# The last batch of a gated MLP with spatial mixing: four pieces of 272 columns instead of 276, and the streamed operands of TensorE moved to other addresses

## The chip, the cores and the metric

One core of a Trainium2 chip. The metric is the device time of one execution in microseconds (us); smaller is better. Three runs of the kernel before took 318.91, 319.26 and 319.99 us, median 319.26 us.

## What is computed

```python
# attention without softmax, B=4 batches, H=4 heads, S=1088 tokens, head_dim 32
phi(x)  = outer(S1 @ x, S2 @ x).reshape(64)
out     = phi(q) @ (phi(k).T @ v) / (phi(q) @ sum(phi(k)) + 1e-6)
x       = heads joined                                  # [B, 1088, 128]
# gated MLP, d_ff = 1024
h       = relu(x @ w_in); u, v = h[..., :512], h[..., 512:]
v_n     = layer norm of v
v_s     = einsum('ts,bsd->btd', w_spatial, v_n) + b_spatial   # W is 1088 x 1088
result  = (u * v_s) @ w_out                             # [B, 1088, 128]
```

Everything must hold to float32 accuracy, so each large product is made of float32r matmuls on a high and a low part: a·b is a_hi·b_hi + a_lo·b_hi + a_hi·b_lo, three matmuls.

## The kernel before

The work runs batch after batch. While TensorE (PE) mixes the tokens of batch b, the attention of batch b+1 is prepared on the other engines and put between its matmuls. The order of every operation on every engine is a list of numbers in the source (ORDER, one number for each recorded operation); the program issues them in that order and adds the semaphores.

**W.** Transposed W lies in SBUF as tile wT, high parts (wTh) and low parts (wTl), 9 row blocks of 128 tokens (NS), a row of PITCH = 1152 floats. Its 1088 columns are three chunks CH, chunk 1 with 332 columns, chunk 0 with 424, chunk 2 with 332. AT tells where each lies in a row: chunk 1 at 0, chunk 0 at 332, then a gap of 12 floats (GAP, filled with zeros by two POOL operations at L584), and chunk 2 at 768.

**Batches 0 to 2** (main, L927 on) take the columns by these chunks: for each d (four blocks of 128 features) and chunk, hidden makes u (3 matmuls into bank pu), spatial runs 26 matmuls into bank sp (L1041, L1043, L1050, L1052), gate multiplies and splits (DVE, ACT), and out_mm multiplies by w_out (3 matmuls into bank po). In each of these matmuls the streamed ("moving") operand is a row of 332 or 424 floats: of wT in spatial, of x in hidden, of the tile g in out_mm. The 128 x 128 operand that is loaded first ("stationary") is a block of v, w_in or w_out.

**The last batch** (main_fast, L1216 on) makes the mixing of two feature blocks with 7 block products instead of 8: W is cut into 2 x 2 blocks, 512 tokens by half of the columns, and sums of such blocks are made ahead from W's columns, which are loaded again from HBM (weights_fast: block, L1172; halves, L1182; less after it). Each half is two pieces CW of 276 columns:

```python
CW = (276, 276)
FROM = ((0, 276), (548, 824))
```

The last 64 tokens are a remainder of two matmuls (L1325, L1326). Since 1088 columns and the gap of 12 are cut into four pieces of 276, the third piece (548 to 823) holds 4 columns that the second has too, 204 columns, the gap, and 56 columns. REAL says which of its columns are real: hidden and out_mm use 260 there, and gate multiplies it in two parts, 204 and 56 columns. All in all main_fast issues 464 matmuls, 336 in product (L1313 to L1315), 32 in the remainders, 48 in hidden (helper L460 to L462), 48 in out_mm (L1402 to L1404); 440 of them stream 276 columns, 24 stream 260.

**Where the operands lie.** All tiles have fixed places in SBUF, one after the other in the order in which the code asks for them, so the start of each streamed operand modulo 64 bytes can be worked out. The code has small pads (pad0 to pad4, and `[:, 4:]` on wT) that shift these starts by 16 or 32 bytes. In the kernel before they are:

| streamed operand | columns | start modulo 64 bytes |
|---|---|---|
| wT, chunks 1 and 2; g | 332 | 48 |
| wT, chunk 0; g, chunk 0 | 424 | 32 |
| x, chunk 1; x, chunk 2 | 332 | 32; 48 |
| x, chunk 0 | 424 | 16 |
| last batch: wT, block sums, x, gates | 276, 260 | 0, 16, 32 and 48, mixed |

The stationary operands start at 32 modulo 64, but for those of attention's 384- and 320-column matmuls (0) and four of the last batch's remainders (48).

Of the kernel before, what the change touches and what calls it, by code (L numbers as in the profile page):

```python
# [9 lines left out]
F32 = mybir.dt.float32  # L10
F32R = mybir.dt.float32r
# [8 lines left out]
P = 128  # L20
# [10 lines left out]
AT = [332, 0, 768]  # L31
PITCH, G_PITCH, G_AT = 1152, 448, {424: 0, 332: 52}
GAP = slice(756, 768)
CW = (276, 276)
FROM = ((0, 276), (548, 824))
HALF = sum(CW)
REAL = (((0, [(0, 276)]), (276, [(0, 276)])), ((552, [(4, 204), (220, 56)]), (812, [(0, 276)])))
SEGS = (0, 276, 332, 548, 552, 768, 824, 828, 1104)
# [51 lines left out]
0 1 2 3 4 5 10 13 14 11 6 12 15 56 37 7 8 16 17 18 19 20 21 22 59 60 61 43 44 45 39 po0 47 48 49 27 28 29 30 31 32 23 po1 po1 po1 po1 68 41 51 69 52 58 70 65 38 40 53 42 57 202 46  # L90
50 66 9 24 54 71 62 203 211 178 193 187 175 102 63 33 101 207 190 181 67 55 103 34 72 35 64 81 82 73 74 75 92 79 76 90 212 36 213 204 214 80 77 78 215 91 83 194 188 179 116 117 112
120 84 216 85 217 86 218 118 113 93 87 219 88 94 114 121 119 182 89 115 95 122 104 191 176 96 123 141 124 220 125 97 133 126 105 142 143 134 352 127 353 189 135 128 144 137 129 138
139 136 366 367 98 99 205 221 106 100 206 210 208 109 131' 381 184 382 154 140 130 145 285 132 177 146 147 286 162 396 148 155 291 163 297 180 107 199 149 292 158 159 290 287 289
293 150 108 196 164 288 294 295 298' 296 302 299 301 300 160 165 156 152 157 161 151' 303 153' 185 304 166 167 168 169 170 171 305 307 306 308 309 315 172' 200 321 222 310 312 311
313 197 195 316 314 320 186 322 318 183 173' 327 192 174 326 317 333 323 319 325 328 249 336 255 256 324 329 338 331 332 341 209 372 339 330 373 342 374 375 387 223 201 340 388 389
# [1475 lines left out]
```

## Time and profile before

| | |
|---|---|
| median of three runs | 319.26 us |
| the profiled execution: its own time | 319.49 us |
| its span, first to last instruction | 317.7 us |
| PE busy | 312.8 us, 98% of the span |
| DVE, ACT, POOL busy | 237.7, 172.9, 48.4 us |
| granted TensorE clock | 0.999, full speed (2.4 GHz) |

The profile calls a matmul busy from its start to the modelled end of its pipeline, and matmuls overlap. The busy time of one (290 ns for 276 columns) is thus not what it costs in a stream; that is the distance from its start to the start of the next, which the timeline shows.

### The profile page before, as it was taken

To read this page: it belongs to the slowest core of one execution; us is meant where nothing else is said; L and a number is where in the kernel's file an instruction comes from. 1 tells how busy PE (TensorE), PEld (TensorE's weight loads), DVE (VectorE), ACT (ScalarE), POOL (GpSimd) and SP (SyncE) were. 2 spreads that over 40 slices of the span, in tenths; PEclk is the share of its full clock that TensorE was granted. 3 is DMA by queue.
4 is the path that set the end of the run, shared out by engine and by line. 5 is a ranking of instruction groups with operands and counts; after the bars stand their busy time and mean duration, and the time that the engine had idled before them with its cause. 6 is when DMAs were issued, how large, how long until landed. Compare 5 with 4: busy or idle time off the path is not lost.

```text
span 317.7 us, 7096 instructions
## 1 busy us (share of the span) xinstructions
PE 312.8 (98%) x2717; PEld 299.4 (94%) x2717; DVE 237.7 (75%) x551; ACT 172.9 (54%) x424; POOL 48.4 (15%) x63
## 2 busy tenths in 40 slices
PE   8999999999999999999999999999999999999996
PEld 7877999999999999999889999999999999999995
DVE  5999997365787956468895789879987987863445
ACT  2599956445774354465636557653154468442432
POOL 2000100765500001642002342100000000000000
PEclk9999999999999999999999999999999999999999
DMA  6952255637113036620113432423121333210001
GB/s 192 325 164 55 77 173 179 210 114 217 45 52 96 12 99 163 166 79 0 50 33 109 138 115 78 121 59 85 53 73 53 92 99 108 78 39 2 0 2 70
DMA packets 26019, 30.77 MB, mean 97 GB/s; under 512 B 3330, under 2 KB 25730, under 8 KB 25986
## 3 DMA queue, kind: packets, MB, share of 16 engines
q1 hardware_dynamic: 25986, 30.33, 32.2%
q8 instruction: 21, 0.34, 0.5%
q14 instruction: 12, 0.10, 0.1%
HBM read 27.25 MB, written 3.06 MB: 95 GB/s over the span
## 4 chain that ended last, share of the span: by engine, by line
PE 95%; DMA 3%; DVE 1%; SPq 1%; issue 0%; DVEq 0%
PE sp L1041 16%; PE sp L1043 14%; PE sp L1050 14%; PE sd L460 4%; PE sd L461 4%; PE sd L462 4%; PE pu L460 3%; PE sd L1313 3%; PE sd L1315 3%; PE sd L1314 3%; PE pu L461 2%; PE pu L462 2%; PE po L460 2%; PE sp L1313 2%; PE sp L1315 2%; PE sp L1314 2%
## 5 line engine op out<-in xcount | busy, mean ns | idle before, releaser
L1041 PE MATMUL sp<-wT,vh 128*128 128x332 f32 (+1 forms) x306 | 98.9, 324 | 0.0
L1043 PE MATMUL sp<-wT,vl 128*128 128x332 f32 (+1 forms) x272 | 87.7, 322 | 0.0
L1050 PE MATMUL sp<-wT,vh 128*128 128x332 f32 (+1 forms) x272 | 86.0, 321 | 0.0
L1041 PEld LDWEIGHTS sp<-wT,vh 128*128 128x128 f32 x306 | 57.5, 188 | 1.8 <-issue 0.8
L1043 PEld LDWEIGHTS sp<-wT,vl 128*128 128x128 f32 x272 | 51.1, 188 | 0.6
L1050 PEld LDWEIGHTS sp<-wT,vh 128*128 128x128 f32 x272 | 51.1, 188 | 0.1
L1077 DVE TENSOR_TENSOR u<-sp,u 128x332 f32<-128x332 f32 (+1 forms) x32 | 16.7, 522 | 17.9 <-PE sp L1052 7.9
L899 DVE BATCH_NORM_STATS2 small<-vt 128x6 f32<-128x512 f32 x36 | 24.1, 682 | 6.7 <-ACT vt L897 6.7
L897 ACT ACTIVATE vt<-sd 128x512 f32<-128x512 f32 x36 | 21.4, 599 | 11.7 <-PE sd L462 10.9
L877 DVE RECIPROCAL area<-area 128x384 f32<-128x384 f32 (+1 forms) x9 | 21.8, 2419 | 7.0 <-ACT area L875 7.0
L816 POOL TENSOR_TENSOR area<-area 128x384 f32<-128x384 f32 (+1 forms) x18 | 17.3, 970 | 57.6 <-DVE vh L966 26.5
L543 ACT CAST g<-u 128x332 fp32r<-128x332 f32 (+1 forms) x32 | 15.5, 487 | 18.0 <-DVE u L1077 9.4
L1033 ACT ACTIVATE u<-pu 128x332 f32<-128x332 f32 (+1 forms) x32 | 14.9, 466 | 11.0 <-PE pu L462 9.7
L473 POOL TENSOR_TENSOR area<-area,area 128x384 fp32r<-128x384 f32 (+1 forms) x18 | 18.0, 1005 | 19.5 <-ACT area L543 10.8
L470 DVE TENSOR_TENSOR g<-u,g 128x332 fp32r<-128x332 f32 (+1 forms) x32 | 17.1, 533 | 2.4 <-ACT g L543 1.4
L630 DVE TENSOR_TENSOR area<-ka,sd 128x768 f32<-128x768 f32 x15 | 13.7, 946 | 4.7 <-ACT ka L628 4.6
L595 ACT CAST wT<-area 128x332 fp32r<-128x332 f32 (+1 forms) x27 | 12.4, 497 | 8.0 <-DMA area<-in_wT 7.9
L460 PE MATMUL pu<-x,wih 128*128 128x332 f32 (+3 forms) x52 | 16.7, 320 | 0.0
L461 PE MATMUL pu<-x,wih 128*128 128x332 f32 (+3 forms) x52 | 16.3, 314 | 0.0
L462 PE MATMUL pu<-x,wil 128*128 128x332 f32 (+3 forms) x52 | 16.3, 314 | 0.0
L919 DVE TENSOR_SCALAR vt<-vt,small 128x512 f32<-128x512 f32 x31 | 15.9, 536 | 0.0
L957 ACT CAST vh<-vt 128x384 fp32r<-128x384 f32 x24 | 12.1, 516 | 6.8 <-DVE vt L919 6.8
(240 smaller groups left out, 765.4 us busy)
## 6 DMA issues: line engine op xcount, KB each, us to landing
w<-in_wT SPq DMA_DIRECT2D x48, 138.0 KB
area<-in_wT SPq DMA_DIRECT2D x18, 166.0 KB
area<-in_vA SPq DMA_DIRECT2D x12, 198.0 KB
area<-in_kT SPq DMA_DIRECT2D x12, 192.0 KB
area<-abd SPq DMA_DIRECT2D x24, 96.0 KB
area<-abd SPq DMA_DIRECT2D x12, 192.0 KB
area<-in_wT SPq DMA_DIRECT2D x9, 212.0 KB
area<-in_qT SPq DMA_DIRECT2D x7, 192.0 KB
```

The lines of the kernel that those rows point to most:

```text
L460: nc.tensor.matmul(o, ah, bh, start=start, stop=False)
L461: nc.tensor.matmul(o, ah, bl, start=False, stop=False)
L462: nc.tensor.matmul(o, al, bh, start=False, stop=stop)
L470: return lambda: nc.vector.tensor_tensor(out=o(), in0=a(), in1=bb(), op=ALU.subtract)
L473: return lambda: nc.gpsimd.tensor_tensor(out=o(), in0=a(), in1=bb(), op=ALU.subtract)
L816: op("POOL", c_pool(n), lambda fa=fa, fb=fb: nc.gpsimd.tensor_tensor(out=fa[:, :n], in0=fa[:, :n], in1=fb[:, :n], op=ALU.mult), r=[fb], w= ...
L877: op("DVE", 135 + 6.3 * n, lambda x32=x32, n=n: nc.vector.reciprocal(out=x32[:, :n], in_=x32[:, :n]), w=[x32])
L897: op("ACT", c_act(512, True) + 16, lambda pv=pv, t=t: nc.scalar.activation(vt[:, t], pv.ap, AF.Relu), r=[pv], w=[(vt, toks(t))])
L899: op("DVE", 690, lambda stats=stats, t=t: nc.vector.bn_stats(out=stats.ap, in_=vt[:, t]), r=[(vt, toks(t))], w=[stats])
L1041: nc.tensor.matmul(sp[:, :cw], vh[:, kt], wTh[:, kt, cs], start=(kt == 0), stop=False)
L1043: nc.tensor.matmul(sp[:, :cw], vl[:, kt], wTh[:, kt, cs], start=False, stop=False)
L1050: nc.tensor.matmul(sp[:, :cw], vh[:, kt], wTl[:, kt, cs], start=False, stop=False)
```

## The change

It cuts the 1088 columns into four pieces of exactly 272 (0, 272, 544, 816), with no gap, no column taken twice, and no partial piece. Chunk 2 of wT moves from 768 to 756. The two POOL operations that zero the gap go. Tiles g, x, the block sums and two stationary tiles (vd0, vd1) are shifted by a few floats.

```diff
-AT = [332, 0, 768]
-PITCH, G_PITCH, G_AT = 1152, 448, {424: 0, 332: 52}
-GAP = slice(756, 768)
-CW = (276, 276)
-FROM = ((0, 276), (548, 824))
+AT = [332, 0, 756]
+PITCH, G_PITCH, G_AT = 1152, 448, (0, 4, 8)
+CW = (272, 272)
+FROM = ((0, 272), (544, 816))
 HALF = sum(CW)
-REAL = (((0, [(0, 276)]), (276, [(0, 276)])), ((552, [(4, 204), (220, 56)]), (812, [(0, 276)])))
-SEGS = (0, 276, 332, 548, 552, 768, 824, 828, 1104)
+SEGS = (0, 272, 332, 544, 756, 816, 1088)
...
-    homes["x"] = const.tile([P, 2, SB_BUFS["xh"], SPAD], F32R, name="x")
+    wide = 2 * SB_BUFS["xh"] * SPAD
+    homes["x"] = const.tile([P, 24 + wide], F32R, name="x")[:, 12:12 + wide].rearrange("p (n i c) -> p n i c", n=2, i=SB_BUFS["xh"])
...
-    homes["vd1", 0] = homes["wi1"][:, HALF + CW[0]:HALF + CW[0] + P]
+    homes["vd1", 0] = homes["wi1"][:, 840:840 + P]
...
-            homes.update({("gf", i): flat[:, i * CW[1]:(i + 1) * CW[1]] for i in range(4)})
-            homes["vd0", 0] = flat[:, 4 * CW[1]:4 * CW[1] + P]
+            homes.update({("gf", i): flat[:, 4 + i * CW[1]:4 + (i + 1) * CW[1]] for i in range(4)})
+            homes["vd0", 0] = flat[:, 1104:1104 + P]
...
-            at = G_AT[t.shape[1]]
-            return homes["g"][:, t.slot, at:at + t.shape[1]]
+            at = t.slot * G_PITCH + G_AT[int(t.name[-1])]
+            return homes["g"][:, at:at + t.shape[1]]
...
-    for t in (wTh, wTl):
-        def blank(t=t):
-            z = z9[:, :NS * 12].rearrange("p (k c) -> p k c", k=NS)
-            return nc.gpsimd.tensor_tensor(out=t[:, :, GAP], in0=z, in1=z, op=ALU.subtract)
-        op("POOL", 360, blank, r=[z9], w=[tl(None, f"gap_{t.name}", [1, 1]), (t, "gap")], due=8000)
...
-                parts = [(lambda: g[:, 0, :cw], (g, 0)), (lambda: g[:, 1, :cw], (g, 1))]
+                parts = [(lambda: g[:, 0, 12:12 + cw], (g, 0)), (lambda: g[:, 1, 12:12 + cw], (g, 1))]
...
-        at = [0, 0, 0]
+        at = [4, 12, 12]
...
         def real(half, c):
-            at, parts = REAL[half][c]
-            return at, sum(n for _, n in parts), parts
+            return FROM[half][c], CW[c], [(0, CW[c])]
```

The starts modulo 64 bytes are then:

| streamed operand | columns | start modulo 64 bytes |
|---|---|---|
| wT, g, x of chunk 1 | 332 | 48 |
| wT, g, x of chunk 2 | 332 | 0 |
| wT, g, x of chunk 0 | 424 | 32 |
| last batch: all 464 matmuls | 272 | 48 |

The stationary operands of the last batch all start at 32 modulo 64. Those of the 512-column matmuls of hidden_v, which are taken from x, move from 32 to 48.

The list ORDER is rewritten from end to end, since six operations go and all later numbers fall. PE, ACT and SP issue what they issued before in the same order, with 272 columns where 276 or 260 stood. On DVE four operations less are issued, all in the last batch. One place of DVE's order there before (w, u, g, vt are tiles in SBUF, sd a PSUM bank, the number behind a name tells its buffer; at the end of a row stand partitions by elements):

```order
L1378 TENSOR_TENSOR w_2260<-sd_93,w_2260 128x276
L1390 TENSOR_TENSOR u_250<-w_2260,u_250 128x204
L1138 TENSOR_TENSOR g<-u_243,g 128x276
L1390 TENSOR_TENSOR u_250<-w_2260,u_250 128x56
L1138 TENSOR_TENSOR vt<-vt 128x4x128 x2
L1138 TENSOR_TENSOR w_2254<-w_2254,w_2258 128x276
```

and with the change:

```order
L1370 TENSOR_TENSOR w_2258<-sd_93,w_2258 128x272
L1380 TENSOR_TENSOR u_250<-w_2258,u_250 128x272
L1131 TENSOR_TENSOR g<-u_243,g 128x272
L1131 TENSOR_TENSOR vt<-vt 128x4x128 x2
L1131 TENSOR_TENSOR w_2252<-w_2252,w_2256 128x272
```

One multiplication of 272 columns stands where two of 204 and 56 stood. The other place of this kind is POOL's start of the work on W, before:

```order
L500 CAST v_87<-first 64x128
L988 ISA
L988 TENSOR_TENSOR vl<-vt,vh 128x512
L584 TENSOR_TENSOR wT<-first 128x9x12 x2
L598 TENSOR_TENSOR wT<-area_79,wT 128x332 x5
L816 TENSOR_TENSOR area_79<-area_79 128x384
```

and with the change:

```order
L500 CAST v_87<-first 64x128
L981 ISA
L981 TENSOR_TENSOR vl<-vt,vh 128x512
L591 TENSOR_TENSOR wT<-area_79,wT 128x332 x5
L809 TENSOR_TENSOR area_79<-area_79 128x384
```

The two operations that zero the gap are gone, and nothing else moved.

## Rows read from the trace of the kernel before

**Rows 1.** The page: span, busy time by engine, the chain that ended last.

```profile
span 317.7 us, 7096 instructions
PE 312.8 (98%) x2717; PEld 299.4 (94%) x2717; DVE 237.7 (75%) x551; ACT 172.9 (54%) x424; POOL 48.4 (15%) x63
PE 95%; DMA 3%; DVE 1%; SPq 1%; issue 0%; DVEq 0%
```

**Rows 2.** Windows: busy us (xcount) of PE, PEld, DVE, ACT, POOL; clock; DMA.

```profile
254.80:314.60 59.80, 59.80 (x468) 59.26 (x466) 38.36 (x94) 28.80 (x80) 0.00 (x0) 1.00 0.16 47
```

**Rows 3.** Timeline of PE, last batch: start us, busy us, line, operands, columns.

```profile
282.83 0.29 PE L1315 MATMUL sp<-later,vh 128*128 128x276 f32 x1
...
286.13 0.29 PE L1313 MATMUL sd<-wT,vh 128*128 128x276 f32 x1
...
307.77 0.28 PE L460 MATMUL pu<-x,wih 128*128 128x260 f32 x1
...
308.13 0.29 PE L1313 MATMUL sd<-wT,vh 128*128 128x276 f32 x1
```

**Rows 4.** Timeline of PE, a stream of 332 columns at 48 after 512-column matmuls.

```profile
214.05 0.31 PE L1041 MATMUL sp<-wT,vh 128*128 128x332 f32 x1
...
216.79 0.31 PE L1041 MATMUL sp<-wT,vh 128*128 128x332 f32 x1
...
217.67 0.31 PE L1041 MATMUL sp<-wT,vh 128*128 128x332 f32 x1
```

**Rows 5.** Timeline of PE, x of chunk 2 (at 48) inside such a stream.

```profile
233.14 0.31 PE L1050 MATMUL sp<-wT,vh 128*128 128x332 f32 x1
233.29 0.31 PE L460 MATMUL pu<-x,wih 128*128 128x332 f32 x1
...
234.02 0.31 PE L1050 MATMUL sp<-wT,vh 128*128 128x332 f32 x1
```

**Rows 6.** Timeline of PE: x chunk 1 (at 32), 424 columns, x chunk 0 (at 16).

```profile
236.66 0.32 PE L460 MATMUL pu<-x,wih 128*128 128x332 f32 x1
...
237.12 0.35 PE L1041 MATMUL sp<-wT,vh 128*128 128x424 f32 x1
...
238.80 0.36 PE L460 MATMUL pu<-x,wih 128*128 128x424 f32 x1
...
239.97 0.35 PE L1041 MATMUL sp<-wT,vh 128*128 128x424 f32 x1
```

**Rows 7.** Timeline of PE, DVE and ACT around the tightest supply in the last batch.

```profile
269.15 0.29 PE L1314 MATMUL sp<-later,vl 128*128 128x276 f32 x1
268.32 0.68 DVE L1138 TENSOR_TENSOR vl<-vt,vh 128x512 fp32r<-128x512 f32 x1
262.28 0.39 ACT L1368 COPY w<-sd 128x276 f32<-128x276 f32 x1 [1.68 <-PE sd L1315]
```

**Rows 8.** Operations of DVE and POOL that go: by form, and POOL's timeline.

```profile
L1390 DVE TENSOR_TENSOR u<-w,u 128x204 f32<-128x204 f32 x2 | 0.7, 371 | 0.2
L1390 DVE TENSOR_TENSOR u<-w,u 128x56 f32<-128x56 f32 x2 | 0.4, 209 | 0.0
55.32 0.69 POOL L584 TENSOR_TENSOR wT<-first 128x108 fp32r<-128x108 f32 x2 [21.49 <-DVE x L470]
```

**Rows 9.** Timeline of PE, DVE and ACT at the end.

```profile
312.39 0.29 PE L1326 MATMUL sd<-wT,wi 128*128 128x276 f32 x1
312.51 0.29 PE L1402 MATMUL po<-g,woh 128*128 128x276 f32 x1
312.78 0.45 DVE L1384 TENSOR_TENSOR u<-sd,u 128x276 f32<-128x276 f32 x1 [0.18 <-PE sd L1326]
313.26 0.42 ACT L1397 CAST later<-u 128x276 fp32r<-128x276 f32 x1 [0.84 <-DVE u L1384]
313.71 0.45 DVE L1138 TENSOR_TENSOR later<-u,later 128x276 fp32r<-128x276 f32 x1
314.21 0.39 PE L1404 MATMUL po<-later,woh 128*128 128x276 f32 x1
```

More of the change, by code (lines that the diff above doesn't have):

```diff
@@ L89 @@
 ORDER = """
[L90 to L95, printed above, removed]
[42 rows of a table removed]
+0 1 2 3 4 5 10 13 14 11 6 12 15 54 35 7 8 16 17 18 19 20 21 22 57 58 59 41 42 43 37 po0 45 46 47 25 26 27 28 29 30 23 po1 po1 po1 po1 66 39 49 67 50 56 68 63 36 38 51 40 55 200
+44 48 64 9 24 52 69 60 201 209 176 191 185 173 100 61 31 99 205 188 179 65 53 101 32 70 33 62 79 80 71 72 73 90 77 74 88 210 34 211 202 212 78 75 76 213 89 81 192 186 177 114
+115 110 118 82 214 83 215 84 216 116 111 91 85 217 86 92 112 119 117 180 87 113 93 120 102 189 174 94 121 139 122 218 123 95 131 124 103 140 141 132 350 125 351 187 133 126 142
+135 127 136 137 134 364 365 96 97 203 219 104 98 204 208 206 107 129' 379 182 380 152 138 128 143 283 130 175 144 145 284 160 394 146 153 289 161 295 178 105 197 147 290 156
+157 288 285 287 291 148 106 194 162 286 292 293 296' 294 300 297 299 298 158 163 154 150 155 159 149' 301 151' 183 302 164 165 166 167 168 169 303 305 304 306 307 313 170' 198
+319 220 308 310 309 311 195 193 314 312 318 184 320 316 181 171' 325 190 172 324 315 331 321 317 323 326 247 334 253 254 322 327 336 329 330 339 207 370 337 328 371 340 372 373
[43 rows of a table added]
 """
@@ L371, in tile_kernel @@
     const.tile([P, 4], F32, name="pad3")
-    first = const.tile([P, SB_BUFS["g"] * G_PITCH], F32, name="first", tag="garea", bufs=1)
+    first = const.tile([P, SB_BUFS["g"] * G_PITCH - 24], F32, name="first", tag="garea", bufs=1)
     fixed["z9"], fixed["sk_e"] = first[:, :P], first[:, P:P + NSK]
-    homes["x"] = const.tile([P, 2, SB_BUFS["xh"], SPAD], F32R, name="x")
+    wide = 2 * SB_BUFS["xh"] * SPAD
+    homes["x"] = const.tile([P, 24 + wide], F32R, name="x")[:, 12:12 + wide].rearrange("p (n i c) -> p n i c", n=2, i=SB_BUFS["xh"])
     homes |= {(t, i): homes["x"][:, n, i] for n, t in enumerate(("xh", "xl")) for i in range(SB_BUFS[t])}
@@ L415, in gates @@
         if "g" not in homes:
-            flat = const.tile([P, SB_BUFS["g"] * G_PITCH], F32R, name="g", tag="garea", bufs=1)
-            homes["g"] = flat.rearrange("p (n c) -> p n c", c=G_PITCH)
-            homes.update({("gf", i): flat[:, i * CW[1]:(i + 1) * CW[1]] for i in range(4)})
-            homes["vd0", 0] = flat[:, 4 * CW[1]:4 * CW[1] + P]
+            flat = const.tile([P, SB_BUFS["g"] * G_PITCH - 24], F32R, name="g", tag="garea", bufs=1)
+            homes["g"] = flat
+            homes.update({("gf", i): flat[:, 4 + i * CW[1]:4 + (i + 1) * CW[1]] for i in range(4)})
+            homes["vd0", 0] = flat[:, 1104:1104 + P]
     def place(t):
@@ L424, in place @@
         if t.tag == "ge":
-            return later(0)[:, t.slot * CW[1]:(t.slot + 1) * CW[1]]
+            return later(0)[:, 4 + t.slot * CW[1]:4 + (t.slot + 1) * CW[1]]
         if t.name in ("wTh", "wTl"):
@@ L1155, in weights_fast @@
                     if (j, i, n, c) == (4, 3, 1, 0):
-                        pieces[j, i, n, c] = (lambda: homes["wi1"][:, HALF:HALF + CW[0]]), [(t, (j, i, n, c)) for t in (wih[1], wil[1])]
+                        pieces[j, i, n, c] = (lambda: homes["wi1"][:, 12 + HALF:12 + HALF + CW[0]]), [(t, (j, i, n, c)) for t in (wih[1], wil[1])]
                         continue
@@ L1163, in weights_fast @@
             cs = slice(CW[0] * c, CW[0] * c + CW[c])
-            pieces[2, 1, 1, c] = (lambda cs=cs: homes["wi1"][:, cs]), [(t, (2, 1, 1, c)) for t in (wih[1], wil[1])]
+            pieces[2, 1, 1, c] = (lambda cs=cs: homes["wi1"][:, 12 + cs.start:12 + cs.stop]), [(t, (2, 1, 1, c)) for t in (wih[1], wil[1])]
             for i in range(4):
@@ L1168, in weights_fast @@
                         pieces[2, i, n, c] = (lambda i=i, n=n, cs=cs: sx[i - 2][:, n * HALF + cs.start:n * HALF + cs.stop]), [(sx[i - 2], (n, c))]
-                    t, a = (wTh, wTl)[n], SEGS[4] + CW[0] * c
+                    t, a = (wTh, wTl)[n], FROM[1][c]
                     pieces[3, i, n, c] = (lambda i=i, t=t, a=a, c=c: t[:, i, a:a + CW[c]]), [(t, cols(i, a, CW[c]))]
```

85 rows, old and new, of the table ORDER are left out of this document.

## The prediction

> **What bounds the kernel now.** The page comes first. PE is busy 98% of the span, and PE is 95% of the chain that ended last [rows 1]. The windows say it for the last batch: from 254.80 to 314.60 us PE is busy all of the 59.80 us, in 468 matmuls, at the full clock, while DVE fills 38.36 us and ACT 28.80 [rows 2]. So what counts is how long one matmul holds PE, and the timeline tells it as the distance between starts. In the last batch the first and the last start shown are 26 matmuls of 276 columns apart: (286.13 − 282.83) / 26 = 126.9 ns [rows 3]. A matmul of 260 columns holds it (308.13 − 307.77) / 3 = 120 ns [rows 3].
>
> The reader should then compare these with the columns alone, at 2.4 per ns: 276 columns are 115.0 ns, so 11.9 ns are extra, 10.3%. In a long stream of 332 columns (138.3 ns) the extra is smaller, but only after a while. From 214.05 to 216.79 are 18 matmuls of 152.2 ns (extra 10%), and the next six, to 217.67, have 146.7 ns (extra 6.0%) [rows 4]. I call the first state unsettled and the second settled. Nothing differs between them but the time since the stream began: the same line, tile and address. For 424 columns (176.7 ns) nine settled matmuls, 237.12 to 238.80, have 186.7 ns (extra 5.7%) [rows 6].
>
> Two things decide whether a stream settles. The first is the start address. Three matmuls on x of chunk 2, which start at 48 modulo 64 as the stream around them does, cost (234.02 − 233.14) / 6 = 146.7 ns on average, so they don't disturb it [rows 5]. Three on x of chunk 1, at 32 between streams at other addresses, cost (237.12 − 236.66) / 3 = 153 ns [rows 6]. Three on x of chunk 0, at 16, cost with the three of out_mm that follow them (239.97 − 238.80) / 6 = 195 ns instead of 186.7 [rows 6]. The second is the length. 146.7 ns are 22 steps of 6.67 ns (16 columns' time at 2.4 GHz), and 186.7 are 28 such steps. A stream settles, as I read it, where the time that a matmul wants, about 1.06 of its columns' time, is a whole number of such steps, so that the next one starts as the last did. For 276 columns, 1.06 × 115.0 = 121.9 ns lies between 18 steps (120.0) and 19 (126.7): they can't settle, and have 126.9.
>
> **The change, part by part.**
>
> (a) *The last batch.* All 464 matmuls get 272 columns and one start, 48. Their columns take 113.3 ns, and 1.06 × 113.3 = 120.1 ns is 18 steps. No row shows 272 columns. The bounds: below, the ratio of settled 424 (186.7 / 176.7), 119.8 ns; above, the ratio of 276 now (126.9 / 115.0), 125.1 ns. I take 120.0, since 332 and 424 settle within a percent of that ratio where the steps fit. 440 matmuls go from 126.9 to 120.0. The six of them that start after 312.39 don't count, since there PE waits for the last gate [rows 9]: 434 × 6.9 = 3.0 us less. The 24 of 260 columns stay at 120 ns: 0.
>
> (b) *Supply.* With PE faster, what is late next? The closest delivery is at 269.15, where PE takes the low part that DVE finished at 268.32 + 0.68 = 269.00 [rows 7]; 0.15 us of room. PE would come about 122 matmuls × 6.9 ns = 0.84 us earlier. ACT's and DVE's work for it hangs on a PE result at 262.28 [rows 7], which itself comes 0.47 us earlier. That leaves 0.84 − 0.47 − 0.15 = 0.2 us of waiting. Bounds: 0 and 0.7 (if DVE doesn't move). +0.2 us.
>
> (c) *The 332-column streams of batches 0 to 2.* This is the price. Until now all of wT and g at 332 columns starts at 48; with the change chunk 1 starts at 48 and chunk 2 at 0, and the order puts them in turn. In the order of PE's queue the 768 matmuls of 332 columns stand in 39 unbroken runs of one address now and in 101 with the change, 62 more, most of them of 3 matmuls. An unsettled matmul costs 152.2 − 146.7 = 5.5 ns more [rows 4]; three of them 16.5 ns; 62 × 16.5 = +1.0 us. Below, 0: a move by 16 bytes might cost nothing at equal length. Above, if nothing at 0 ever settles: 384 × 5.5 = +2.1 us.
>
> (d) *x of chunk 0 goes from 16 to 32*, the address of its stream. The six matmuls at 195 ns cost 6 × 8.3 = 50 ns more than settled ones [rows 6]; I count only the three on x, since the stream after them is often cut by something else anyway: 25 ns for each of 11 such runs, −0.27 us. Bounds: −0.1 (the stream is unsettled there in most places) and −0.55 (all six).
>
> (e) *What costs nothing.* POOL's two zeroings took 0.69 us at 55.32 after 21.49 us of idling [rows 8]; the cover is POOL's 15% load. DVE loses four operations; (371 + 209) ns become some 445 [rows 8, 9], 0.5 us in all on an engine with a third of the last batch free [rows 2]. The end, from the remainder's matmul at 312.39 through DVE 0.45, ACT 0.42, DVE 0.45 to the last matmul and its store [rows 9], has 4 columns less in each: under 0.02 us. The 512-column matmuls keep their moving operand; their stationary one goes from 32 to 48, and no row shows whether that counts.
>
> Sum: −3.0 + 0.2 + 1.0 − 0.27 = −2.1 us. The profiled execution took 319.49 us, 0.23 over the median of 319.26; against the median the forecast is **317.2 us**.
>
> **The rivals.**
>
> *Only columns count.* [...] As a mechanism of this kernel: from 260 to 276 columns the distance grows by 6.9 / 16 = 0.43 ns a column [rows 3], so 272 take 125.2. The gain is 440 × 1.7 − 24 × 5.2 = 0.6 us, the other streams stay: **318.6 us**. Against it stands the drop from 152.2 to 146.7 at equal columns [rows 4]. Chance 0.12.
>
> *272 doesn't settle*, because what it wants is a little over 18 steps (by a line through the settled 332 and 424, whose extras are 8.3 and 10.0 ns, it would be 120.6). Then it takes about 125 too, −0.6, and the streams of 332 pay +1.0, less 0.27: **319.4 us**. Chance 0.17.
>
> *Slower: chunk 2 at 0 never settles.* The only rows with starts at 0 and 48 in turn are the mixed 276s, all unsettled. Then (c) is 2.1 us, paid over three batches, and with (d) that is +1.85. It decides for a slower kernel where the last batch brings under 0.9 us, that is where 272 takes over 124.9 ns; at 125.2, **320.5 us**. For it: every new address here is untried. Against it: 424 settles at 32 and 332 at 48, so no single address is needed. Chance 0.09. With 272 settled and chunk 2 not, −3.0 + 0.2 + 2.1 − 0.27 = −1.0, **318.3 us**; chance 0.06.
>
> **How the numbers follow.** The forecast has 0.56. Its own range is 316.2 (switches free, no waiting) to 317.9 (0.7 us of waiting or dearer switches). To hold 8 in 10, I reach to 319.6, over the first two rivals and the last; 320.5 and some hundredths below 316.2 are left out. A measurement tells about 0.3% (0.96 us) from no change, so faster is below 318.3. Faster: the forecast and half of the 318.3 case, 0.59, say 0.60. Same: 318.6, 319.4 and the other half, 0.31. Slower: 0.09.
>
> **What would show it.** In the timeline of the changed kernel the last batch's starts should be 120.0 ns apart within some 15 matmuls and stay so; 125 would prove (a) wrong, and with it most of the forecast. The window of the 468 matmuls should last some 57 us instead of 59.80. A run at 0 of more than 15 matmuls at 332 columns should come down to 146.7 ns; if it stays at 152, the slower rival's mechanism is there. Three-matmul groups at a foreign address should cost about 152 each. A gap before a matmul near 266 to 269 us, released by DVE, would show (b). The end behind the last remainder should keep its length.

## The result, and the profile after

The changed kernel took 321.3 us (median of six runs, 320.76 to 322.0), the kernel before 319.14 us beside it (six runs). The ratio is 1.0064, with a 95% interval of 1.0047 to 1.0081: **slower by some 0.6%**, where 317.2 us and a gain of 0.6% had been forecast. 321.3 lies above the range too. The profiled execution took 322.0 us.

The page of the changed kernel looks like the one before [rows 1]: PE is still the bound, and its busy time grew by 1.1 us.

```profile
span 320.2 us, 7086 instructions
PE 313.9 (98%) x2717; PEld 300.7 (94%) x2717; DVE 236.8 (74%) x547; ACT 172.9 (54%) x424; POOL 47.7 (15%) x61
PE 96%; DMA 2%; SPq 1%; DVE 0%; issue 0%
```

The window of the last batch, with the same 468 matmuls as [rows 2], comes 3 us later and is only 0.6 us shorter, not 3:

```profile
257.95:317.15 59.20, 59.20 (x468) 58.69 (x466) 37.86 (x90) 28.75 (x80) 0.00 (x0) 1.00 0.16 47
```

The timeline of PE tells why. Columns: start us, busy us, line, operands, columns streamed. First, 26 matmuls out of the last batch. From the first start shown to the second it is (286.08 − 282.82) / 26 = 125.4 ns for one. The forecast was 120.0; the 276 columns before had 126.9 [rows 3].

```profile
282.82 0.29 PE L1308 MATMUL sp<-later,vh 128*128 128x272 f32 x1
...
286.08 0.29 PE L1308 MATMUL sp<-later,vh 128*128 128x272 f32 x1
```

Now two long streams of 332 columns, the first on W's chunk 1 (start 48 modulo 64), 37 matmuls, the second on chunk 2 (start 0), 26 matmuls, each up to the next operand:

```profile
62.19 0.31 PE L1034 MATMUL sp<-wT,vh 128*128 128x332 f32 x1
...
67.61 0.32 PE L460 MATMUL po<-g,woh 128*128 128x332 f32 x1
...
205.22 0.32 PE L1034 MATMUL sp<-wT,vh 128*128 128x332 f32 x1
...
209.20 0.31 PE L460 MATMUL pu<-x,wih 128*128 128x332 f32 x1
```

(67.61 − 62.19) / 37 = 146.5 ns: settled from its first matmul. (209.20 − 205.22) / 26 = 153.1 ns: not settled to its end, though 26 matmuls are more than the 18 after which the stream of [rows 4] came down.

Where the time went: from the first 512-column matmul to the first one of the last batch the kernel before took 235.24 us, the changed one 237.51: **+2.27**. From there to the last matmul 60.49 and 59.79: **−0.70**. The sums of the distances by length agree with the first: all matmuls of 332 columns took 2.56 us more, all of 424 columns 0.12 less, all of 512 columns 0.10 less. The two stretches together make +1.57 of the 2.16 us between the medians. The first 512-column matmul itself started 0.97 us later in this profile; in the eleven profiles of the whole program in this study it starts anywhere from 17.78 to 19.46 us, the changed kernel's being the latest, and the chain up to it holds nothing that was changed. The 0.6 us that remain may come from that, or from chance: the interval of the ratio reaches from 1.5 to 2.6 us, and 1.57 lies within it.

### The profile page after: what moved, and what is told of

It is laid out like the page before. It is cut to its first block, busy times and chain, and to the rows that moved or that the text cites. A ratio compares the mean times of both kernels' runs of the same rounds, so it can differ in the third digit from the quotient of the medians.

```text
span 320.2 us, 7086 instructions
## 1 busy us (share of the span) xinstructions
PE 313.9 (98%) x2717; PEld 300.7 (94%) x2717; DVE 236.8 (74%) x547; ACT 172.9 (54%) x424; POOL 47.7 (15%) x61
## 4 chain that ended last, share of the span: by engine, by line
PE 96%; DMA 2%; SPq 1%; DVE 0%; issue 0%
PE sp L1034 16%; PE sp L1036 14%; PE sp L1043 14%; PE sd L460 4%; PE sd L461 4%; PE sd L462 4%; PE pu L460 3%; PE sd L1306 3%; PE sd L1307 3%; PE sd L1308 2%; PE pu L462 2%; PE pu L461 2%; PE po L460 2%; DMA area<-in_idn 2%; PE sp L1308 2%; PE sp L1306 2%
## 5 line engine op out<-in xcount | busy, mean ns | idle before, releaser
L460 PE MATMUL pu<-x,wih 128*128 128x332 f32 (+2 forms) x52 | 16.7, 321 | 0.0
L462 PE MATMUL pu<-x,wil 128*128 128x332 f32 (+2 forms) x52 | 16.3, 314 | 0.0
L461 PE MATMUL pu<-x,wih 128*128 128x332 f32 (+2 forms) x52 | 16.3, 314 | 0.0
```

Source lines behind the costliest of these rows:

```text
L460: nc.tensor.matmul(o, ah, bh, start=start, stop=False)
L461: nc.tensor.matmul(o, ah, bl, start=False, stop=False)
L462: nc.tensor.matmul(o, al, bh, start=False, stop=stop)
```

## The experiments

How to read what follows: for each matmul the distance from its own start to the next one's, averaged over all of one kind in a trace; distances over 1.25 times the columns' time are left out, since there PE waited. Which chunk a matmul belongs to, and where its operands start, follows from the source, whose order of matmuls is that of the trace. "Settled" is a distance of at most 147 ns for 332 columns and 187 for 424. From experiment 5 on there is a second kind of distance, in bytes: from the start of the stationary tile to the start of the streamed operand, modulo 128.

**1. Four addresses for each length.** One kernel is the kernel before with W moved by 16 bytes; three are the changed kernel with all streamed operands moved by 16, 32 and 48 bytes.

```diff
 (before, W by 16 bytes)
-homes["wT"] = const.tile([P, 4 + 2 * NS * PITCH], F32R, name="wT")[:, 4:]
+homes["wT"] = const.tile([P, 8 + 2 * NS * PITCH], F32R, name="wT")[:, 8:]
 (changed, by 16, 32, 48 bytes: sh = 4, 8, 12; likewise g, the pieces in the areas and wi1)
-... name="wT")[:, 4:]             ... name="x")[:, 12:12 + wide]
+... name="wT")[:, 4 + sh:]        ... name="x")[:, 12 + sh:12 + sh + wide]
```

> The kernel before with W's rows alone moved by 16 bytes: its 624 streams of 332 columns on W start at 0 modulo 64 instead of 48, all at one address, in the long unbroken runs that the kernel before has; its 312 streams of 424 columns on W go from 32 to 48. Theory A (whether a length settles hangs on its own start address): the long runs of 332 stay near 153 ns as in the changed kernel's chunk 2, and never reach 146.7; 624 times some 5 ns is +3 us, about 322 us. Rival B (what keeps a stream from settling is that addresses alternate): the long runs at 0 settle at 146.7 ns as those at 48 did, and the time stays within 1 us of the kernel before, 319 to 320 us. What 424 columns do at 48 is not forecast by B beyond no change; A allows either 186.7 or about 194 ns (312 times 7 ns, another +2 us).

> The changed kernel with every streamed operand moved by 16 bytes: 272 columns at 0 modulo 64, 332 at 0 (chunk 1) and 16 (chunk 2), 424 at 48. Theory A (length and own address): 332 of chunk 1, now at 0, stays near 153 ns where it had 149 at 48; 272 may settle at 120.0 ns here or not. Rival B (alternation): nothing changes, since the differences between addresses are the same; 321.3 us as the changed kernel. Rival C (272 is too long for 18 steps of 6.67 ns at any address): 272 stays at 125 ns in all four of the shifts 0, 16, 32 and 48.

> The changed kernel with every streamed operand moved by 32 bytes: 272 columns at 16 modulo 64, 332 at 16 (chunk 1) and 32 (chunk 2), 424 at 0. Theory A: 272 settles at 120.0 ns at one of the four addresses (464 times 5 ns, 2.3 us less); 332 at 32 near 153 as x of chunk 1 had there in the kernel before. Rival B: 321.3 us, no change. Rival C: 272 at 125 ns here too.

> The changed kernel with every streamed operand moved by 48 bytes: 272 columns at 32 modulo 64, 332 at 32 (chunk 1) and 48 (chunk 2), 424 at 16. Theory A: 332 of chunk 2, now at 48, comes down to about 149 ns and settles at 146.7 in long runs, while chunk 1, at 32, goes up to 153; 424 at 16 unsettled, about 194 ns as x of chunk 0 had there before. Rival B: 321.3 us, no change. Rival C: 272 at 125 ns here too.

Measured: 322.74 us (ratio 1.0112, 1.0095 to 1.0129), 323.0 (1.0123, 1.0101 to 1.0144), 322.81 (1.0117, 1.0099 to 1.0135) and 321.36 us (1.0068, 1.0045 to 1.009). Rival B falls on the first: in the kernel before with W alone moved, 43 matmuls in a row at one address never settle, (224.74 − 218.24) / 43 = 151.2 ns.

```profile
218.24 0.31 PE L1041 MATMUL sp<-wT,vh 128*128 128x332 f32 x1
...
224.74 0.32 PE L460 MATMUL po<-g,woh 128*128 128x332 f32 x1
```

So it is not alternation that keeps 332 columns at 0 from settling. 272 columns had 125.1, 125.7, 125.2 and 125.6 ns from 48, 0, 16 and 32: none settles. 424 settled from 32 alone. For these two lengths theory A holds so far. For 332 it fails already here: in the fourth kernel it had chunk 1, at 32 modulo 64, going up to 153 ns, and chunk 1 has 149.1; chunk 2, at 32 in the third, has 151.8, and no two of its matmuls on W in a row are settled. One length at one start modulo 64 has two values.

**2. PE alone.** Two kernels compute nothing of the reference: PE streams rows of 23 or 24 matmuls of one length from one start, while nothing else runs.

```python
for n in LENGTHS:                       # 29 lengths; the second kernel: 332, 424, 272
    for start in (32, 48, 0, 16):       # within a tile that itself begins at 32 modulo 128
        stream(n, start, 24)            # the second kernel: one matmul of another length, then 23
```

> A measurement by itself, with nothing of the reference's computation: PE alone streams 24 matmuls in a row of one length from one start address, stationary tiles taken in turn from eight at 32 modulo 64 as in the kernel, for 29 lengths from 256 to 432 columns and the starts 32, 48, 0 and 16. Theory A (length and own start decide, also without other engines): 332 settles at 146.7 ns from 32 and from 48 and stays near 153 from 0; 424 settles at 186.7 ns from 32 alone and stays near 193 from 0, 16 and 48; 272 has 125 ns from all four. A's reading of the steps: settled is columns / 16 plus about 1.25, rounded up to whole steps of 6.67 ns, so 268 columns (16.75 + 1.25 = 18 steps) might have 120.0 ns from some address and 348 (21.75 + 1.25 = 23) 153.3. Rival D (the extra over the columns comes from DVE's, ACT's and POOL's traffic on the same memory): with PE alone no address differs from another, and every length has one distance, at or below the settled one.

> A measurement by itself, with nothing of the reference's computation: PE alone streams 23 matmuls in a row of 332, 424 or 272 columns from each of the eight starts 0, 16, ... 112 modulo 128; every row of 23 is entered through one matmul of another length (256, 260, 264 or 268 columns), which shifts the moment at which it begins; and 332 and 272 from 16 and 48 with stationary tiles at 32, 48 and 0 modulo 64. Theory A (length and own start modulo 64 decide): the four entries agree, 48 and 112 agree, 332 is at 146.7 ns from 48 and 112 after each entry and at 152 to 153 from 0 and 64. Theory E (a row of matmuls falls into one of several repeating patterns on a grid of 6.67 ns, and which one hangs on the moment it begins as well as on the address): the same length and start gives different distances after different entries, 146.7 and 150 to 153 for 332, 186.7 and 190 to 193 for 424. By both, 272 reaches 120.0 nowhere. If the stationary tile's address counted, 332 from 48 would lose its 146.7 ns at 48 or 0.

Measured, as the mean of the last twelve distances of a row: in the first kernel 332 columns had 151.9, 153.3, 150.0 and **146.7** ns from 64, 80, 32 and 48 modulo 128, and 424 had 192.3, 193.3, 193.3 and **186.7**. Rival D falls: addresses differ with no other engine at work. In the two kernels 272 has 42 rows, from all eight starts modulo 128, between 123.3 and 126.7 ns: it settles nowhere. Theory A's reading of the steps fails with it: 268 and 348 columns, which it singled out for 120.0 and 153.3 ns, have 123.3 and 158.3 at best. And its modulo 64 breaks once more. In the second kernel 424 had 186.7 ns from 48 after all four entries, and 193.3 from 112 after all four, although 48 and 112 are equal modulo 64. Thirteen matmuls of such a row, from 48 and then from 112, take 2.59 and 2.67 us to the end of the last:

```profile
159.79 2.59 PE L47 MATMUL bank<-m,w 128*128 128x424 f32 x13
...
141.78 2.67 PE L47 MATMUL bank<-m,w 128*128 128x424 f32 x13
```

With the stationary tiles at other places 332 changed its distances at one and the same start. And theory E is partly right: 332 from 48 had 146.7 ns after one entry and 152.0 to 152.1 after the three others. A row falls into a repeating pattern, and more than one is possible.

**3. Undoing one part.** First chunk 2 back at 48 modulo 64, and, in the same comparison, x alone moved in the kernel before (with batch 0's gated pieces of chunk 0, which lie in the same tile).

```diff
 (changed kernel: W and x of chunk 2 read 4 columns early, in spatial and hidden; g alike)
-cs = slice(AT[c], AT[c] + cw)
+cs = slice(AT[c] - 4 * (c == 2), AT[c] - 4 * (c == 2) + cw)
 (before: x by 16 bytes)
-homes["x"] = const.tile([P, 2, SB_BUFS["xh"], SPAD], F32R, name="x")
+homes["x"] = const.tile([P, 16 + 4 * SPAD], F32R, name="x")[:, 4:4 + 4 * SPAD]...
```

> The changed kernel with one part undone: in batches 0 to 2 every stream of chunk 2 (W, x and the gated pieces) starts at 48 modulo 64 again instead of 0. W and x are read four columns early for that, so chunk 2 of these batches is computed from the wrong columns; all lengths, orders and the last batch stay. If chunk 2's start is what costs, the 332-column matmuls fall from 153.3 to about 148 ns, their sum from 114.6 to 112.0 us, and the time from 321.3 to 318.7 us, 0.4 us under the kernel before (the last batch's 0.7 less the start-up difference). If the alternation is not the price but something else in the change (the last batch, the shifts of x and g), the time stays at 321 us.

> The kernel before with one part of the change alone: x moved by 16 bytes, so that x of chunk 0 starts at 32 modulo 64, as its stream does, instead of 16 (chunk 1 at 48, chunk 2 at 0). The prediction's term (d): 0.27 us less, 318.9 us, with x of chunk 0 near 187 to 189 ns instead of 192.9; below that, x of chunk 2 at 0 among streams at 48 gives back what x of chunk 1 gains. If patterns hang on the moment of entry more than on the address, no difference, 319.2 us.

Measured: 320.54 us (1.004, 1.0025 to 1.0055), not 318.7; and 319.04 us (1.0, 0.9988 to 1.0012). The first misses its time. The time of the second tells nothing, since 0.27 us less lies within its interval; but x of chunk 0 misses its 187 to 189 ns. Both misses have one reason. The run of 26 on chunk 2 that was shown at 205.22 has (206.98 − 203.06) / 26 = 150.8 ns here, not settled, though it starts at 48 modulo 64 as chunk 1 does:

```profile
203.06 0.31 PE L1034 MATMUL sp<-wT,vh 128*128 128x332 f32 x1
...
206.98 0.32 PE L460 MATMUL pu<-x,wih 128*128 128x332 f32 x1
```

Modulo 128 it starts at 48, and chunk 1, like both chunks in the kernel before, at 112. Likewise x of chunk 0, moved by 16, starts at 96 and not at 32 modulo 128, and keeps 192.4 ns (192.9 before). That the second kernel's time is unchanged is a sum of two moves: its 332s on x took some 0.3 us more (chunk 2's went from 147.2 to 153.8 ns at their new start), and all its 424s 0.65 us less, since W's chunk 0 went from 189.5 to 187.3 ns at an unchanged address. Why it did stays open.

**4. Modulo 128.** The same undoing with chunk 2 at 112 modulo 128, and, against it, a move that changes nothing modulo 64.

```diff
 (changed kernel: 20 columns early instead of 4; g of chunks 1 and 2 at 112 too)
+cs = slice(AT[c] - 20 * (c == 2), AT[c] - 20 * (c == 2) + cw)
 (changed kernel: W, g and x 64 bytes further)
+homes["wT"] = const.tile([P, 20 + 2 * NS * PITCH], F32R, name="wT")[:, 20:]
```

> The changed kernel with one part undone, the undoing now made modulo 128: in batches 0 to 2 every stream of chunk 2 (W, x and the gated pieces) starts at 112 modulo 128, where W's chunk 1 and, in the kernel before, both chunks start; the gated pieces of chunk 1 go from 48 back to 112 too. W and x are read twenty columns early for that, so chunk 2 of these batches is computed from the wrong columns; all lengths, orders and the last batch stay. Theory F (the start address counts modulo 128: 332 settles from 112 and not from 48, 64 or 0): some 80% of the 332s settle, their sum falls from 114.6 to 112 us, and the time to about 318.7 us. Rival (modulo 64 is what counts, and the change's two kinds of streams disturb each other): as with the start at 48, near 320.5 us.

> The changed kernel with W, x and the gated pieces of batches 0 to 2 moved by 64 bytes: modulo 64 no start differs from the changed kernel's; modulo 128 chunk 1 goes from 112 to 48, chunk 0 from 32 to 96, chunk 2 from 64 to 0. If modulo 64 counts, 321.3 us as the changed kernel, with chunk 1 at 149 and chunk 0 at 189.5 ns. Theory F (modulo 128): chunk 1 loses its settled state, 348 matmuls times 3 ns, and 424 at 96 unsettled, 376 times 3 ns: 2.2 us more, 323.5 us.

Measured: 319.0 us (0.9995, 0.9985 to 1.0005) and 323.05 us (1.0125, 1.0103 to 1.0148). Of the first, the same run of 26: (206.56 − 202.72) / 26 = 147.7 ns, settled after four. Theory F had some 80% of the 332s settled and a sum of 112 us; 60 and 65% of those on W's chunks 1 and 2 settled, and the sum fell from 114.6 to 112.8. Modulo 256 these two chunks lie 128 bytes apart in this kernel, and they settle alike.

```profile
202.72 0.32 PE L1034 MATMUL sp<-wT,vh 128*128 128x332 f32 x1
...
206.56 0.31 PE L460 MATMUL pu<-x,wih 128*128 128x332 f32 x1
```

Of the second, the run of 37 on chunk 1 that had 146.5 ns at 62.19 of the changed kernel: (66.82 − 61.19) / 37 = 152.2 ns, at an equal start modulo 64.

```profile
61.19 0.31 PE L1034 MATMUL sp<-wT,vh 128*128 128x332 f32 x1
...
66.82 0.32 PE L460 MATMUL po<-g,woh 128*128 128x332 f32 x1
```

The rule by which the change equalized addresses is refuted: it counted modulo 64, and a move by 64 bytes alone cost 1.75 us.

**5. Start, or distance from the stationary tile?** In all kernels of experiments 1, 3 and 4 the stationary tiles of these streams stood at 96 modulo 128 (but for a few of them), so the two could not be told apart. In the kernel before everything was moved by 32 bytes; a last kernel has PE alone once more.

```diff
 (before)
-const.tile([P, 8], F32, name=f"pad{i}")
+const.tile([P, 8 + 8 * (not i)], F32, name=f"pad{i}")
```

> The kernel before with everything in SBUF moved by 32 bytes, streamed operands and stationary ones alike: 332 columns start at 16 modulo 128 instead of 112, 424 at 64 instead of 32, the stationary tiles at 0 instead of 96. Theory F (the streamed operand's own start modulo 128 decides): 332 from 16 and 424 from 64 never settled in the runs so far (152.1 and 194.0 ns with the stationary tiles at 96), so both lose it: 624 times 4.5 ns and 312 times 3.5 ns, +3.9 us, 323 us. Theory G (the distance from the stationary tile's start to the streamed operand's start modulo 128 decides; 16 and 64 are the distances at which streams settled, in the kernels as with PE alone): the distances stay 16 and 64, and the time stays 319.2 us, with W's 332 columns at 147.6 ns on average.

> A measurement by itself, with nothing of the reference's computation: PE alone, rows of 23 matmuls. First 15 lengths from 320 to 448 columns from the starts 112 and 32 modulo 128 with the stationary tiles at 96, each entered through one matmul of 256 and of 260 columns; then 332 and 424 columns from all eight starts with the stationary tiles at 0 and at 48. Theory G (distance modulo 128 from the stationary tile's start): with the stationary tiles at 0, 332 and 424 reach 146.7 and 186.7 ns only from 16 or 64; with them at 48, only from 64 or 112. Theory F (own start): the same starts as with them at 32 before, 48 and 96, in both. Of the other lengths it asks which settle at the distances 16 and 64 (columns / 16 plus at most 1.5 steps of 6.67 ns).

Measured: 318.65 us against 318.81 (0.9996, 0.9979 to 1.0012), as theory G said, and not 323. Its run of 26, at a start (16) that had not settled with the stationary tiles at 96, has (205.68 − 201.83) / 26 = 148.1 ns, and the same run in the kernel before 148.0. Of the 936 distances in ns of W's matmuls 95% are equal in the two traces to within 1 ns, those at the unsettled beginnings of runs included.

```profile
201.83 0.32 PE L1041 MATMUL sp<-wT,vh 128*128 128x332 f32 x1
...
205.68 0.31 PE L460 MATMUL pu<-x,wih 128*128 128x332 f32 x1
```

All of W's streams, by the distance of their start from the stationary tile's start modulo 128 (mean ns; chunk 1 / chunk 2 / chunk 0):

| kernel | distances | 332, chunk 1 | 332, chunk 2 | 424 |
|---|---|---|---|---|
| before | 16 / 16 / 64 | 147.3 | 147.8 | 189.5 |
| changed | 16 / 96 / 64 | 148.5 | 153.3 | 189.5 |
| before, W by 16 bytes | 32 / 32 / 80 | 152.1 | 151.9 | 192.8 |
| changed, by 16 bytes | 32 / 112 / 80 | 152.4 | 152.1 | 192.9 |
| changed, by 32 bytes | 48 / 0 / 96 | 152.2 | 151.8 | 194.0 |
| changed, by 48 bytes | 64 / 16 / 112 | 149.1 | 148.9 | 193.9 |
| chunk 2 four columns early | 16 / 80 / 64 | 148.5 | 151.7 | 189.3 |
| chunk 2 twenty columns early | 16 / 16 / 64 | 148.6 | 148.5 | 189.4 |
| changed, W, g, x by 64 bytes | 80 / 32 / 0 | 152.1 | 152.2 | 192.8 |
| before, all by 32 bytes | 16 / 16 / 64 | 147.3 | 147.5 | 189.5 |

At 16 and 64 (424 columns: at 64, the only one of the two that W's chunk 0 had) streams settle, in rows of 20 matmuls and more. At the other distances no two of W's matmuls in a row are settled, but for 332 columns at 112 (in the changed kernel moved by 16 bytes a quarter of them, in rows of up to 23). With PE alone, in all three kernels, 332 columns settled in 3 of 9 rows at 16, 4 of 10 at 64 and 1 of 6 at 112, 424 in 8 of 9 at 16 and 3 of 8 at 64; at the other distances neither settled in any of 76 rows. Part of the last expectation missed: with the stationary tiles at 48, 332 reached 146.7 ns from 112 but not from 64, and 424 from neither; with them at 0, 332 settled at the distance 112 too. The distance allows the settled state; whether a row reaches it hangs on more. The entry is one thing (332 columns at 16 and 64 in the second kernel). It is not all: after an entry of 256 columns, 424 settled at 16 with the stationary tiles at 0, 32 and 96, and not with them at 48. What else counts stays open. Of the 13 other lengths, none from 320 to 448 came under 1.069 times its columns' time there (332: 1.060, 424: 1.057).

Could a layout keep both gains? Without a gap, chunks of 332, 424 and 332 columns lie at distances o, o + 48, o + 80 modulo 128, or in another order at o, o + 48, o + 96 or o, o + 32, o + 80: one of the three always falls beside 16 and 64. Little would be gained by it: the kernel with chunk 2 read twenty columns early has the 272 columns and all 332s at 16, and its ratio to the kernel before is 0.9995. No version here beats the kernel before.

## Why the prediction was wrong, step by step

**(a) failed: the last batch.** "120.1 ns is 18 steps": 272 columns were to settle because 332 and 424 do at that ratio. They have 125.1 ns in the changed kernel, and settled in none of four more layouts nor in 42 rows with PE alone. The upper bound of the step, 125.1, was the value. The last batch gave 0.70 us, not 3.0. This was the larger part of the miss: 2.3 us of the forecast. The rule behind the step, that a length settles where 1.06 times its columns' time is a whole number of steps, was read off two lengths. 348 columns should settle by it as well, at 23 steps or 153.3 ns, and had 158.3 at best; and of the 34 lengths besides 332 and 424 that PE ran alone, 272 among them, none came under 1.069 times its columns' time. The one start for all 464 matmuls brought next to nothing: four columns less are 1.7 ns, and 276 columns went from 127.0 ns on average to 125.1. Why 332 and 424 settle and 272 does not, no run here shows.

**(c) failed: the 332-column streams.** The step counted 62 switches at 16.5 ns, +1.0 us, with 2.1 as the bound "if nothing at 0 ever settles". The bound was the case, and a little more: all 332s together took 112.0 us before and 114.6 after, +2.6. Those of chunk 2 (W, x and g, 384 in all) went from 147.8 to 153.3 ns on average, +2.1 us. Those of chunk 1 went from 147.8 to 149.0, +0.5 us: on W, at an unchanged address, from 147.3 to 148.5, and their settled share fell from 85 to 62%. It would be near at hand to take this for the price of switching, which the step had counted. The kernel with chunk 2 read twenty columns early speaks against it: all its 332s have one start, nothing switches, and chunk 1 has 148.6 ns and 60% there too (148.5 and 67% with chunk 2 read four columns early, which switches). No run shows a price of switching, and what chunk 1 lost stays unexplained. Behind the step stands a reading that was wrong ahead of the sum. I took starts modulo 64 for what the streams see, because the diff did; experiments 4 and 5 show the distance to the stationary tile modulo 128. The changed kernel moved chunk 2 from the distance 16 to 96. With it back at 16 the time was 319.0 us. Two readings of rows fall with that. x of chunk 1, which seemed to show a bad start [rows 6], lay at 64, one of the two good distances. And of the 18 unsettled matmuls of [rows 4], taken for one line and tile, three are on g, at the same start.

**(d) held in kind, half in size.** x of chunk 0 went from 112 to 64 bytes in distance and from 192.9 to 190.1 ns. Three of its matmuls and the three after them, inside a settled stream: (213.73 − 212.61) / 6 = 186.7 ns, where [rows 6] had 195.

```profile
212.61 0.35 PE L460 MATMUL pu<-x,wih 128*128 128x424 f32 x1
...
213.73 0.35 PE L1034 MATMUL sp<-wT,vh 128*128 128x424 f32 x1
```

All 424s together gained 0.12 us; 0.27 was forecast, with 0.1 as the lower bound.

**(b) did not arise.** DVE ends the low part at 271.46 + 0.68 = 272.14, and PE takes it at 272.21, without a wait; 0.07 us of room are left of the 0.15 in [rows 7]. Whether DVE would have been late cannot be told: PE never came the 0.84 us earlier that the step presumed, since (a) failed.

```profile
272.21 0.29 PE L1307 MATMUL sp<-later,vl 128*128 128x272 f32 x1
271.46 0.68 DVE L1131 TENSOR_TENSOR vl<-vt,vh 128x512 fp32r<-128x512 f32 x1
```

**(e) held.** PE is 96% of the chain that ended last (95% before), DVE 0%, and POOL is not in it: the operations that went had held nothing up. The 512-column matmuls, left open there, went from 233.5 to 232.4 ns, 0.1 us in all. The end, from the remainder's last matmul through DVE, ACT, DVE to PE's last, has 316.75 − 314.94 = 1.81 us, and had 314.21 − 312.39 = 1.82 [rows 9].

```profile
314.94 0.28 PE L1319 MATMUL sd<-wT,wi 128*128 128x272 f32 x1
...
315.33 0.44 DVE L1376 TENSOR_TENSOR u<-sd,u 128x272 f32<-128x272 f32 x1 [0.15 <-PE sd L1319]
...
315.80 0.42 ACT L1389 CAST later<-u 128x272 fp32r<-128x272 f32 x1 [0.80 <-DVE u L1376]
...
316.26 0.44 DVE L1131 TENSOR_TENSOR later<-u,later 128x272 fp32r<-128x272 f32 x1
...
316.75 0.39 PE L1396 MATMUL po<-later,woh 128*128 128x272 f32 x1
```

**The rivals.** The one on the slower side, "chunk 2 at 0 never settles", is what happened, in mechanism and nearly in time: 320.5 us, with a chance of 0.09. Its point of decision was right: slower where 272 takes over 124.9 ns. Its chance was too low because the argument against it ("424 settles at 32 and 332 at 48, so no single address is needed") took two working addresses as a sign that a third would work; of the eight distances two work well. "272 doesn't settle" was right on the last batch (0.6 us there, 0.70 measured) and wrong on the price of the 332s; the slower rival is the two together. "Only columns count" is refuted by experiment 4: equal columns, 1.75 us apart. For the last batch alone its 0.6 us were near.

## What to carry to other kernels

Where PE is the bound, compare the distance between matmul starts with the columns' time; an extra of 10% against 6% of it is worth looking for. Before an operand is moved, measure the new place for that length in the kernel itself, with its stationary tile's place written beside it: a rule that fits two working addresses says nothing of a third. A padding or a gap that seems idle (here 12 columns of zeros) may hold an operand at the place where it streams fast.

## What was not expected of the hardware

- A stream of matmuls runs faster or slower by some 3.5% with the distance, modulo 128 bytes, between the start of the streamed operand and that of the stationary tile: 332 columns 146.7 or some 152 ns, 424 columns 186.7 or 193.3. The Trainium skill's page "TensorE: Matmul & The Clock Gate", section "Step-by-step: what each phase is for", says that PE reads the streamed operand and the weights through two independent ports, so that loading the next weights takes nothing from the running matmul. The 3% between the kernel before with W alone moved (152.0 ns) and with all moved alike (147.4) speak against full independence; which part of the memory they share no run here shows.
- With PE alone most rows ended in a pattern that repeats exactly, with a mean of a whole number of steps of 6.67 ns or a simple fraction: 22, 22.5, 22.67 or 23 steps for 332 columns. Which one was reached also hung on the length of the one matmul before the row.
- Still open: why W's chunk 1 settles in 85% of its matmuls before, and in 60 to 67% in the changed kernel and the two with chunk 2 read early, although its own address is the same in all four.
